# An mLSTM cell with a cosine-gated MLP: the second product by seven half-width block products for eight

## The chip, the cores and the metric

The kernel runs on one core of a Trainium2 chip. The metric is the device time of one execution in microseconds, taken as the median over several runs. The engines are PE (TensorE matmuls; PEld is its weight load), DVE (VectorE), ACT (ScalarE), POOL (GpSimd) and SP (SyncE, which here issues the DMAs). Each engine works off its own instructions strictly in the order in which they were emitted; engines wait for each other through semaphores.

## What is computed

Two stages follow each other. The first is an mLSTM cell over 4 batches, 8 heads, 768 steps and head size 40; the second takes its output as 3072 tokens of width 320 through two matrix products with 2048 hidden columns.

```
for t in range(S):
    m_new = np.maximum(f_gate[:, :, t] + m, i_gate[:, :, t])
    f_stab = np.exp(f_gate[:, :, t] + m - m_new)
    i_stab = np.exp(i_gate[:, :, t] - m_new)
    m = m_new
    C = f_stab[..., None, None] * C + i_stab[..., None, None] * einsum('bhd,bhe->bhde', v_t, k_t)
    n = f_stab[..., None] * n + i_stab[..., None] * k_t
    y[:, :, t] = sigmoid(o_t) * (C q_t) / max(|n . q_t|, 1)
x = y as (4*768, 320)
h = x @ w_in             # 320 x 2048
g = h * cos(h)
out = g @ w_out          # 2048 x 320
```

## The kernel before

The 768 steps are cut into 6 chunks of 128 (`C`), and the cell is computed chunk by chunk in its parallel form: within a chunk by a 128x128 matrix of weights per head, between chunks through a state of 40x48 per head. A *cell* is one chunk of one batch, number n = 4c + b, with all 8 heads, so there are 24 cells. The MLP works on a chunk c of all four batches at once: 512 tokens. The hidden width is cut into 16 blocks of 128 (`f`), taken two at a time, so a chunk has 8 *slots* (`f2` from 0 to 7).

`first_cells` computes the four cells of chunk 0. Then `both_parts(c, b)` runs for every chunk and batch: two slots (i = 0 and 1) of the MLP on chunk c, with the cell of batch b of chunk c + 1 woven in between. The order in which it calls its parts is the order on every engine (the block is under a manual schedule). In chunk 5 there is no cell left to weave in.

A slot with i = 0 emits: `Up` (L605, L608: the first product into two PSUM banks `pup`, six matmuls); `scores` of the cell (L462); for `g` the ACT step `near` (L613) and the DVE step `rest` (L616); `weigh` (L468: scores times decays `E`, DVE); `decay_exponents` of the next cell (L387 DVE subtraction, L388 POOL mask); `sin` (L621, ACT) and `gate` (L625, DVE), which writes `g`; in the first slot of a chunk `sigmoid` of the next chunk's output gates (L316, L318, ACT); `decay` of the next cell (L396, ACT exp); then `down` (L637, the second product) for the slot before; then `turn_gate` (L440, DVE transpose), `values` (L488 to L495, into `vt`), `normalize_turned` (L504 to L515, DVE and POOL), `fade` (L550, POOL) and an ACT instruction that loads the sine's table again (L772). A slot with i = 1 emits `Up`, `seam` (L563: the product `px` that turns a part of y into the MLP's layout; L570: the state's update), `near` and `rest`, `seam_out` (L576), `state` (L588, DVE), `sin` and `gate`, `weigh_k` (L401, POOL), `down`, and the transposes of q and k for the next cell (`turn_blocks` L435, `scale_q` L444).

`down(c, f2)` multiplies the two blocks of g by w_out: for each of the four batches a 128x128 block of g is loaded as weights and 320 columns of w_out stream past it, summed over the 16 blocks in the PSUM banks `po`. The last `down` of a chunk runs in slot 0 of the next, and as each batch ends ACT copies it out (L640) into one of two buffers `o_sb`, and SP stores it (L641). A product in float32 is two passes of the PE, each with its own weight load.

The weights come as 8-byte numbers and are turned to float32 in chunk 0 by `to_float32` (L148 to L156: ACT, DVE, POOL). The maxima for the decays come from DRAM as broadcast tiles: `load_E(n)` (L351) fetches E for two cells at once, 1 MB, and `G` (L356) beside it. The buffers `bits` of the weight conversion are four in pool `pb` and three in pool `pc`. Five small tiles of the gate computation (a1, F1, M1, keep, shift) live in the six buffers of `g`.

Of the kernel before, what the change touches and what calls it, by code (L numbers as in the profile page):

```python
# [11 lines left out]
FP = mybir.dt.float32  # L12
# [3 lines left out]
AF = mybir.ActivationFunctionType  # L16
# [13 lines left out]
def kernel(  # L30
# [23 lines left out]
    C = 128  # L54
# [16 lines left out]
    wp = ctx.enter_context(tc.tile_pool(name="wp", bufs=1))  # L71
    p2 = ctx.enter_context(tc.tile_pool(name="p2", bufs=2))
    p3 = ctx.enter_context(tc.tile_pool(name="p3", bufs=3))
    pe = ctx.enter_context(tc.tile_pool(name="pe", bufs=2))
    p1 = ctx.enter_context(tc.tile_pool(name="p1", bufs=1))
    pb = ctx.enter_context(tc.tile_pool(name="pb", bufs=4))
    pc = ctx.enter_context(tc.tile_pool(name="pc", bufs=3))
# [113 lines left out]
    M0 = gates.tile([BH, C], FP, name="M0")  # L191
    e0 = gates.tile([BH, C], FP, name="e0")
    nM = gates.tile([BH, 1], FP, name="nM")
    a1 = gp.tile([128, WQ], FP, name="a1", tag="g")[0:BH].rearrange("r (c s) -> r c s", c=R)
    F1 = gp.tile([128, WQ], FP, name="F1", tag="g")[0:BH].rearrange("r (c s) -> r c s", c=R)
    M1 = gp.tile([128, WQ], FP, name="M1", tag="g")[0:BH].rearrange("r (c s) -> r c s", c=R)

    keep = gp.tile([128, WQ], FP, name="keep", tag="g")[0:BH].rearrange("r (c s) -> r c s", c=R)
    shift = gp.tile([128, WQ], FP, name="shift", tag="g")[0:BH].rearrange("r (c s) -> r c s", c=R)
    m0 = gates.tile([BH, R], FP, name="m0")  # L200
    dd = gates.tile([BH, R - 1, BH], FP, name="dd")
    nc.gpsimd.memset(keep, 1.0)
# [140 lines left out]

    def load_E(n):
        c, b = divmod(n, B)
        E = pe.tile([128, 2, H, C], FP, name="E", tag="E") if n % 2 == 0 else E2[n // 2]
        if n % 2 == 0:
            E2[n // 2] = E
        if c > 0:
            src = M_d[1][b * H:(b + 2) * H, ts(c - 1, C)]  # L350
            nc.sync.dma_start(out=E.rearrange("q b h t -> q (b h) t"), in_=src.unsqueeze(0).to_broadcast([128, 2 * H, C]))  # L351
            Es[n + 1] = E[:, 1]
            G = p2.tile([128, 2 * HP, C], FP, name="G", tag="G")
            src = G_d.rearrange("(b p j) t -> j (b p) t", j=2, p=HP)
            for j in range(2):
                nc.sync.dma_start(out=G[64 * j:64 * j + 64], in_=src[j, 4 * b:4 * b + 8, ts(c - 1, C)].unsqueeze(0).to_broadcast([64, 2 * HP, C]))  # L356
            Gs[n], Gs[n + 1] = G[:, 0:HP], G[:, HP:2 * HP]
        elif n not in SPREAD:
            nc.sync.dma_start(out=E[:, n % 2], in_=M_d[0][ts(b, H)].unsqueeze(0).to_broadcast([128, H, C]))
        Es[n] = E[:, n % 2]  # L360

    E2 = {}
    pm = {}

    def wall_in(n, i, m):
# [18 lines left out]

    def decay_exponents(n):
        E = Es[n]
        nc.vector.tensor_tensor(out=E, in0=E, in1=cols(n, 0, C), op=OP.subtract)  # L387
        nc.gpsimd.affine_select(out=E, in_=E, compare_op=OP.is_ge, fill=1.0e30, base=0,  # L388
                                pattern=[[0, H], [1, C]], channel_multiplier=-1)

# [2 lines left out]
        nc.vector.tensor_tensor(out=Es[n][:, r], in0=pm[n, i], in1=cols(n, 0, C)[:, r], op=OP.subtract)  # L393

    def decay(n):
        nc.scalar.activation(out=Es[n], in_=Es[n], func=AF.Exp, scale=-1.0)  # L396

    def weigh_k(n):
        if n < N - B:
# [100 lines left out]
    def normalize_turned(n):  # L500
        c, b = divmod(n, B)
        vt = heads_of[n]
        dn = p2.tile([128, C], FP, name="dt", tag="dt")
        nc.vector.tensor_scalar(out=dn, in0=vt[:, 2], scalar1=-TWO_PI, scalar2=TWO_PI, op0=OP.mult, op1=OP.max)  # L504
        nc.vector.scalar_tensor_tensor(out=dn, in0=vt[:, 2], scalar=TWO_PI, in1=dn, op0=OP.mult, op1=OP.max)
        yt = p1.tile([128, 3, C], FP, name="yt", tag="yt")
        nc.vector.tensor_tensor(out=yt, in0=vt, in1=oTs[n], op=OP.mult)
        nc.vector.reciprocal(out=dn, in_=dn)
        db = p1.tile([128, 3, C], FP, name="db", tag="db")
        for i, mask in enumerate(([FROM0] * 32, [FROM1] * 32, [FROM0] * 16 + [FROM1] * 16)):  # L510
            nc.vector.stream_shuffle(out=db[:, i], in_=dn, mask=mask)  # L511
        if b == 0:
            xT[c] = p2.tile([128, NK + 1, B, C], FP, name="xT", tag="xT")
        nc.gpsimd.tensor_tensor(out=xT[c][:, 0:NK, b], in0=yt[:, 0:NK], in1=db[:, 0:NK], op=OP.mult)  # L514
        nc.vector.tensor_tensor(out=yt[:, 2], in0=yt[:, 2], in1=db[:, 2], op=OP.mult)  # L515
        ys[n] = yt

    def normalize(n):
        c, b = divmod(n, B)
# [32 lines left out]
    def seam(n):  # L552

        pool, tag = psum(n)
        if n < B:
            px = pool.tile([128, NK + 1, C], FP, name="px", tag=tag)
            for i in range(NK):
                nc.tensor.transpose(px[:, i], ys[n][:, ts(i, 128)], ident)
            for e in range(2):
                nc.tensor.matmul(px[64 * e:64 * e + 64, NK], ys[n][:, KL:DM], ident, start=True, stop=True)  # L560
        else:
            px = pool.tile([128, C], FP, name="px", tag=tag)
            nc.tensor.matmul(px, pick.rearrange("q e g a i -> q (e g a i)"), ys[n][:, 2], start=True, stop=True)  # L563
        pxs[n] = px
        if n < N - B:
            pu = pool.tile([128, HP, DV], FP, name="pu", tag=tag)
            for p in range(HP):
                for j in range(2):
                    h = 2 * p + j
                    nc.tensor.matmul(pu[64 * j:64 * j + D, p], kws[n][:, h, 0:D], vs(n)[:, h], start=True, stop=True)  # L570
            pus[n] = pu
# [21 lines left out]
    class Up:  # L593
# [27 lines left out]
            nc.scalar.activation(out=r, in_=r, func=AF.Sin, scale=TWO_PI_DOWN)  # L621

        def gate(self, e):
            g = gp.tile([128, WQ], FP, name="g", tag="g")[:, 0:B * C]
            nc.vector.scalar_tensor_tensor(out=g, in0=self.pu[e], scalar=TWO_PI, in1=self.n[e].bitcast(FP),  # L625
                                           op0=OP.mult, op1=OP.mult)
            gs[self.c, 2 * self.f2 + e] = g

    def down(c, f2):
        if f2 == 0:  # L630
            po[c] = [ps_o.tile([128, DM], FP, name="po", tag="o") for _ in range(B)]

        order = [(f, b) for f in (2 * f2, 2 * f2 + 1) for b in range(B)]
        if f2 == NF // 2 - 1:
            order.sort(key=lambda fb: fb[1])
        for f, b in order:
            nc.tensor.matmul(po[c][b], gs[c, f][:, ts(b, C)], w_out_sb[:, f], start=(f == 0), stop=(f == NF - 1))  # L637
            if f == NF - 1:
                o = p2.tile([128, DM], FP, name="o_sb", tag="o_sb")
                nc.scalar.copy(out=o, in_=po[c][b])  # L640
                nc.sync.dma_start(out=out[b * S + c * C:b * S + (c + 1) * C], in_=o)  # L641


    pw, pmu = (ps_u.tile([128, HP, C], FP, name=name, tag="up") for name in ("pw", "pmu"))

# [5 lines left out]
    def first_cells():  # L651
# [64 lines left out]
        weigh_k(2)  # L716
        values(1)
        load_E(B)
        last_rows(1)
        load_o(1)  # L720
        outs.append((0, weights_out(0)))
# [58 lines left out]
    def both_parts(c, b):  # L780
# [3 lines left out]
        for i in range(2):  # L784
# [15 lines left out]
            if i == 0:  # L800
                if cell:
                    weigh(n)
                    if n + 1 < N:
                        decay_exponents(n + 1)
                for e in range(2):
                    up.sin(e)
                    up.gate(e)
                if b == 0 and c + 1 < NC:
                    sigmoid(c + 1)

                if c == 0 and b > 0 and pieces:
                    to_float32(*pieces.pop(0))
                if cell and n + 1 < N and (c > 0 or b > 0):
                    decay(n + 1)
            else:
                if cell:
                    seam_out(n)
                if pieces:
                    to_float32(*pieces.pop(0))
                if cell:  # L820
                    state(n)
                for e in range(2):
                    up.sin(e)
                    up.gate(e)
                while pieces:
                    to_float32(*pieces.pop(0))
                if cell and n + 1 < N:
                    weigh_k(n + 1)
                    odd_values(n + 1)
            if f2 > 0:  # L830
                down(c, f2 - 1)
            elif c > 0:
                down(c - 1, NF // 2 - 1)
            if cell and i == 0:
                turn_gate(n)
                values(n)
# [1 line left out]
                fade(n)  # L838
                if n % 2 == 1 and n + 3 < N:
                    load_two(n + 3, "qk")  # L840
                    load_E(n + 3)
                if b == B - 2 and c + 2 < NC:
                    load_o(c + 2)
# [6 lines left out]
            if i == 1:  # L850
                if c == 0 and b + 2 < B:
                    pieces.extend(weights_in(b + 2))
                for _ in range(min(2, len(outs))):
                    next_out()
                if cell and n + 1 < N:
                    turn_blocks(n + 1)
                    scale_q(n + 1)

    pieces, outs = [], []
    with tc.manual_schedule():  # L860
        first_cells()
        for c in range(NC):
            for b in range(B):
                both_parts(c, b)
        down(NC - 1, NF // 2 - 1)


# [28 lines left out]
```

## Time and profile before

| | us |
|---|---|
| runs before | 581.65, 583.64, 583.67 (median 583.64) |
| the profiled execution | 584.48, span 582.6 |
| PE busy | 553.2 (95%) |
| L637, second product | 223.1 |
| L605 and L608, first product | 176.8 and 54.2 |
| DVE busy | 362.9 |
| ACT busy | 257.1 |
| POOL busy | 150.4 |

Busy times of a group of lines count each moment once, so 768 passes of 445 ns mean come to 223.1 us: the passes overlap. In the profile an arrow `<-` inside square brackets gives the idle time before an instruction and what ended it. Granted clock is the share of full TensorE speed that the chip's throttle allowed.

### The profile page before, as it was taken

The numbers are of one execution on the slowest core, as the hardware profiler recorded it, in microseconds if no ns is written. First come the engines' busy times: TensorE is split into PE (matmuls) and PEld (weight loads), VectorE is DVE, ScalarE is ACT, GpSimd is POOL, SyncE is SP. The second block draws the span as 40 slices with busy tenths as digits, with TensorE's granted clock in tenths as the row PEclk, the third lists the DMA queues.
The fourth block names the chain that finished last, engine by engine and source line by source line (L and its number), as shares of the span: only waits on it lengthen the run. The fifth ranks groups of instructions, "written<-read, shape, count | busy, mean of one in ns | idle before, by whom it ended". The sixth has DMA issues, their size and how long they took to land.

```text
span 582.6 us, 8973 instructions
## 1 busy us (share of the span) xinstructions
PE 553.2 (95%) x3404; PEld 325.7 (56%) x3404; DVE 362.9 (62%) x709; ACT 257.1 (44%) x419; POOL 150.4 (26%) x214
## 2 busy tenths in 40 slices
PE   8994959888999999999999999999999999999997
PEld 5862535444556556556556556566566565555454
DVE  5765798978676766766666667666566585423221
ACT  4856526373364344364343373353274251323222
POOL 7523454543231321321321321321211110000000
PEclk9868889997999999999999999999999999999999
DMA  9999999984805924914914914904810000010001
GB/s 149 221 220 216 229 246 228 198 191 90 153 26 112 161 41 91 154 44 93 160 41 90 154 46 92 182 18 90 154 47 2 0 1 1 0 45 1 0 1 45
DMA packets 125866, 58.76 MB, mean 101 GB/s; under 512 B 61648, under 2 KB 122144, under 8 KB 125824
## 3 DMA queue, kind: packets, MB, share of 16 engines
q1 hardware_dynamic: 125680, 58.00, 50.7%
q8 instruction: 27, 0.44, 0.3%
q0 software_dynamic: 96, 0.18, 0.1%
q14 instruction: 15, 0.12, 0.1%
q10 hardware_dynamic: 48, 0.02, 0.0%
HBM read 54.07 MB, written 5.16 MB: 102 GB/s over the span
## 4 chain that ended last, share of the span: by engine, by line
PE 85%; DVE 5%; DMA 5%; SPq 2%; POOL 2%; issue 1%; ACT 0%; POOLq 0%; DVEq 0%; ACTq 0%
PE po L637 35%; PE pup L605 27%; PE pup L608 8%; PE ps L462 4%; PE vt L495 2%; PE vt L488 2%; DMA E<-M_d 2%; DMA o<-in_o_gate_dram 1%; PE px L563 1%; PE pu L570 1%; DMA ks<-in_k_dram 1%; SPq L140 1%; PE ph L478 1%; PE pt L425 1%; DVE w_out_sb L153 1%
## 5 line engine op out<-in xcount | busy, mean ns | idle before, releaser
L637 PE MATMUL po<-w_out_sb,g 128*128 128x320 f32 x768 | 223.1, 445 | 1.0 <-POOL w_out_sb L156 1.0
L637 PEld LDWEIGHTS po<-w_out_sb,g 128*128 128x128 f32 x768 | 144.5, 193 | 65.8 <-issue 9.5
L605 PE MATMUL pup<-xT,w_in_sb 128*128 128x512 f32 x384 | 176.8, 602 | 1.0 <-POOL w_in_sb L156 0.7
L616 DVE SCALAR_TENSOR_TENSOR n<-pup,n 128x512 f32<-128x512 f32 x96 | 61.7, 685 | 157.6 <-ACT n L613 157.5
L613 ACT ACTIVATE n<-pup 128x512 int32<-128x512 f32 x96 | 51.9, 592 | 235.6 <-PE pup L608 235.6
L605 PEld LDWEIGHTS pup<-xT,w_in_sb 128*128 128x128 f32 x384 | 71.7, 192 | 80.3 <-issue 67.0
L621 ACT ACTIVATE n<-n 128x512 f32<-128x512 f32 x96 | 58.6, 630 | 17.4 <-DVE n L616 15.4
L625 DVE SCALAR_TENSOR_TENSOR g<-pup,n 128x512 f32<-128x512 f32 x96 | 61.6, 684 | 1.7
L388 POOL TENSOR_SCALAR_AFFINE_SELECT E<-E 128x1024 f32<-128x1024 f32 x22 | 24.0, 1092 | 129.2 <-DVE E L387 129.2
L608 PE MATMUL pup<-xT,w_in_l 64*128 64x512 f32 x192 | 54.2, 641 | 0.4 <-POOL w_in_l L156 0.4
L444 POOL TENSOR_TENSOR qG<-t,G 128x512 f32<-128x512 f32 x20 | 25.4, 1272 | 67.3 <-DVE t L435 61.7
L514 POOL TENSOR_TENSOR xT<-yt,db 128x256 f32<-128x256 f32 x20 | 14.5, 725 | 92.7 <-DVE db L511 92.7
L396 ACT ACTIVATE E<-E 128x1024 f32<-128x1024 f32 x24 | 25.4, 1060 | 29.3 <-POOL E L388 28.1
L462 PEld LDWEIGHTS ps<-t,t 40*128 40x128 f32 x384 | 26.5, 199 | 21.0 <-issue 17.8
L462 PE MATMUL ps<-t,t 40*128 40x128 f32 x384 | 28.1, 288 | 10.4 <-DVE t L435 10.4
L608 PEld LDWEIGHTS pup<-xT,w_in_l 64*128 64x128 f32 x192 | 14.4, 184 | 36.8 <-issue 34.9
L468 DVE TENSOR_TENSOR E<-ps,E 128x512 f32<-128x512 f32 x48 | 30.7, 680 | 2.4 <-PE ps L462 2.4
L396 ACT ACT_TABLE_LOAD x21 | 26.9, 1283 | 0.4
L387 DVE TENSOR_TENSOR E<-E,tab 128x1024 f32<-128x1024 f32 x22 | 26.7, 1214 | 0.0
L495 PE MATMUL vt<-qG,st 128*32 128x128 f32 x480 | 24.9, 280 | 0.8 <-POOL qG L444 0.8
L772 ACT ACT_TABLE_LOAD x19 | 24.4, 1283 | 0.2
L550 POOL TENSOR_TENSOR st<-st,tab 40x128 f32<-40x128 f32 x64 | 24.1, 395 | 1.2
(140 smaller groups left out, 510.7 us busy)
## 6 DMA issues: line engine op xcount, KB each, us to landing
E<-M_d SPq DMA_DIRECT2D x10, 1024.0 KB, 5.7
qr<-in_q_dram SPq DMA_DIRECT2D x40, 160.0 KB, 3.5
kr<-in_k_dram SPq DMA_DIRECT2D x40, 160.0 KB, 4.8
G<-G_d SPq DMA_DIRECT2D x20, 256.0 KB, 6.8
bits<-in_moe_w_out_dram SPq DMA_DIRECT2D x8, 640.0 KB, 6.6
bits<-in_moe_w_in_dram SPq DMA_DIRECT2D x32, 128.0 KB, 4.6
out_dram<-o_sb SPq DMA_DIRECT2D x24, 160.0 KB, 1.8
o<-in_o_gate_dram SPq DMA_DIRECT2D x40, 80.0 KB, 3.8
```

The costliest lines, as they stand in the source:

```text
L387: nc.vector.tensor_tensor(out=E, in0=E, in1=cols(n, 0, C), op=OP.subtract)
L396: nc.scalar.activation(out=Es[n], in_=Es[n], func=AF.Exp, scale=-1.0)
L462: nc.tensor.matmul(ps[j][:, p], kT[r, p], qT[r, p], start=True, stop=True)
L468: nc.vector.tensor_tensor(out=w, in0=pss[n][j], in1=w, op=OP.mult)
L495: nc.tensor.matmul(vt[32 * a:32 * a + 32, i], state[:, ts(HP * i + a, 32)], Gs[n][:, a], start=False, stop=True)
L605: nc.tensor.matmul(pu, w_in_sb[:, i, ts(2 * f2 + e, 128)], x(i), start=(i == 0), stop=False)
L608: nc.tensor.matmul(pu, w_in_l[r, f2], x(NK, r), start=False, stop=True)
L613: nc.scalar.activation(out=self.n[e], in_=self.pu[e], func=AF.Copy, bias=0.25)
L616: nc.vector.scalar_tensor_tensor(out=self.n[e].bitcast(FP), in0=self.pu[e], scalar=0.25, in1=self.n[e], op0=OP.add, op1=OP.subtract)
L621: nc.scalar.activation(out=r, in_=r, func=AF.Sin, scale=TWO_PI_DOWN)
L625: nc.vector.scalar_tensor_tensor(out=g, in0=self.pu[e], scalar=TWO_PI, in1=self.n[e].bitcast(FP), op0=OP.mult, op1=OP.mult)
L637: nc.tensor.matmul(po[c][b], gs[c, f][:, ts(b, C)], w_out_sb[:, f], start=(f == 0), stop=(f == NF - 1))
```

## The change

For chunks 1 to 5 the second product is done by Winograd's form of Strassen's scheme. Two blocks f of hidden columns and two batches make a 2x2 array of 128x128 blocks of g; w_out's two blocks of rows and its two halves of 160 columns make a 2x2 array of blocks. Seven products of 128x128 by 128x160 replace eight. The sums on the weights' side (`weight_sums`, POOL, 8 operations of 128x640, with T1 in place of B12) are made once: half in slot 7 of chunk 0, half in slot 0 of chunk 1. Those on the side of g (`sums`) are made in every slot of chunks 1 to 5: four additions of 128x128 on DVE for one pair of batches, four on POOL for the other. The products (`products`) are spread over slots 2 to 7 of a chunk and slot 0 of the next (chunk 1 starts in slot 1). They add up in four banks; a fifth (`late`) takes the two products that have no room, in slot 1 of the next chunk, or in another pool's bank for the last chunk. `combine` and `combine_late` put the parts together on ACT and DVE and store them.

Beside that, `decay_exponents` does no subtraction for chunks 1 to 5: the exp on ACT takes the term a as its bias, one head at a time. The scaling of y is one DVE operation of 128x384, where POOL had 128x256 and DVE 128x128. E is fetched for one cell at a time into three buffers (cell 3 borrows a `bits` buffer), the five gate tiles borrow buffers of q, k and `bits`, and `o_sb` has four buffers.

```
     def load_E(n):
...
+        if n == B - 1:
+            E = pb.tile([128, H, C], FP, name="E3", tag="bits")
+        else:
+            E = pe.tile([128, H, C], FP, name="E", tag="E")
+        Es[n] = E
         if c > 0:
+            nc.sync.dma_start(out=E, in_=M_d[1][ts(b, H), ts(c - 1, C)].unsqueeze(0).to_broadcast([128, H, C]))
+            if n % 2 == 1:
+                return
...
     def decay_exponents(n):
         E = Es[n]
-        nc.vector.tensor_tensor(out=E, in0=E, in1=cols(n, 0, C), op=OP.subtract)
+        if n < B:
+            nc.vector.tensor_tensor(out=E, in0=E, in1=cols(n, 0, C), op=OP.subtract)
...
     def decay(n):
...
+        for h in range(H):
+            g = b * H + h
+            nc.scalar.activation(out=Es[n][:, h], in_=Es[n][:, h], func=AF.Exp, scale=-1.0, bias=tab[:, c, 0, g:g + 1])
...
-        nc.gpsimd.tensor_tensor(out=xT[c][:, 0:NK, b], in0=yt[:, 0:NK], in1=db[:, 0:NK], op=OP.mult)
-        nc.vector.tensor_tensor(out=yt[:, 2], in0=yt[:, 2], in1=db[:, 2], op=OP.mult)
-        ys[n] = yt
+        nc.vector.tensor_tensor(out=xT[c][:, :, b], in0=yt, in1=db, op=OP.mult)
+        ys[n] = xT[c][:, NK, b]
...
+    def weight_sums(part):
...
+        nc.gpsimd.tensor_tensor(out=T3, in0=B22, in1=B12, op=OP.subtract)
+        nc.gpsimd.tensor_tensor(out=B12, in0=B12, in1=B11, op=OP.subtract)
+        nc.gpsimd.tensor_tensor(out=T2, in0=B22, in1=B12, op=OP.subtract)
+        nc.gpsimd.tensor_tensor(out=T4, in0=B21, in1=T2, op=OP.subtract)
+    def sums(c, k):
...
+        tt = nc.vector.tensor_tensor
+        tt(out=S[:, 2], in0=G0[:, 0, 1], in1=G1[:, 0, 1], op=OP.add)
+        tt(out=S[:, 0], in0=S[:, 2], in1=G0[:, 0, 0], op=OP.subtract)
+        tt(out=S[:, 3], in0=G1[:, 0, 0], in1=S[:, 0], op=OP.subtract)
+        tt(out=G0[:, 0, 1], in0=G0[:, 0, 0], in1=G0[:, 0, 1], op=OP.subtract)
+        tt = nc.gpsimd.tensor_tensor
+        tt(out=D1, in0=G0[:, 1, 1], in1=G1[:, 1, 1], op=OP.add)
+        tt(out=S[:, 1], in0=D1, in1=G0[:, 1, 0], op=OP.subtract)
+        tt(out=D4, in0=G1[:, 1, 0], in1=S[:, 1], op=OP.subtract)
+        tt(out=G0[:, 1, 1], in0=G0[:, 1, 0], in1=G0[:, 1, 1], op=OP.subtract)
+    def products(c, k):
...
+        made = [(X0, 0, G0[:, 0, 0], B11), (X0, 1, G1[:, 0, 0], B21), (X0, 2, S[:, 0], T2),
+                (Y0, 0, G0[:, 0, 1], T3), (Y0, 1, G1[:, 0, 1], T4), (Y0, 2, S[:, 2], T1),
+                (Y1, 2, S[:, 3], B22),
+                (X1, 0, G0[:, 1, 0], B11), (X1, 1, G1[:, 1, 0], B21), (X1, 2, S[:, 1], T2),
+                (Y1, 0, G0[:, 1, 1], T3), (Y1, 1, G1[:, 1, 1], T4)]
+        if c == NC - 1:
+            L = late[c]
+            made += [(L, 0, D1, T1), (L, 1, D4, B22)]
...
+    def combine(c, p):
...
+        nc.scalar.copy(out=s[:, 0:HALF], in_=X[:, 0])
+        tt(out=o[0].rearrange("q (h n) -> q h n", h=2), in0=X[:, 1:3], in1=s[:, 0:HALF].unsqueeze(1).to_broadcast([128, 2, HALF]), op=OP.add)
+        if p == 0:
...
+            for e in range(2):
+                out_to(c, e, o[e])
+        else:
+            tt(out=o[1][:, HALF:DM], in0=Y[:, 0], in1=o[0][:, HALF:DM], op=OP.add)
+            tt(out=o[1][:, 0:HALF], in0=Y[:, 1], in1=o[1][:, HALF:DM], op=OP.add)
...
+    def down_slot(c, f2):
+        if c == 0:
+            if f2 > 0:
+                down(0, f2 - 1)
+            return
+        if f2 == 0:
+            if c == 1:
+                down(0, LAST)
+            else:
+                run(made_of[c - 1], 12)
+                combine(c - 1, 0)
+                combine(c - 1, 1)
+            return
+        if f2 == 1 and c > 1:
+            run(late_products(c - 1), NF)
+            combine_late(c - 1)
+            return
...
+        each = 14 if c == NC - 1 else 12
+        quota = [0] * 8
+        for m in range(2, 8):
+            quota[m] = each * 7 * (m - 1) // 6 - each * 7 * (m - 2) // 6
+        run(made_of[c], each if c == 1 else quota[f2])
...
     def both_parts(c, b):
...
+                if c > 0:
+                    sums(c, f2)
...
-            if f2 > 0:
-                down(c, f2 - 1)
-            elif c > 0:
-                down(c - 1, NF // 2 - 1)
+            down_slot(c, f2)
+            if (c, f2) == (1, 0):
+                weight_sums(1)
             if cell and i == 0:
                 turn_gate(n)
                 values(n)
                 normalize_turned(n)
                 fade(n)
                 if n % 2 == 1 and n + 3 < N:
                     load_two(n + 3, "qk")
+                if n + 3 < N:
                     load_E(n + 3)
...
+        run(made_of[NC - 1], 14)
+        for p in range(2):
+            combine(NC - 1, p)
+        combine_late(NC - 1)
```

## The prediction

> **What bounds the kernel now.** I read the page first (shares, costliest groups), then the busy times by stage, the chain of waits around the idle gaps, and the instructions in order of time at one change of token chunk.
>
> ```profile
> PE 553.2 (95%) x3404; PEld 325.7 (56%) x3404; DVE 362.9 (62%) x709; ACT 257.1 (44%) x419; POOL 150.4 (26%) x214
> L637 PE MATMUL po<-w_out_sb,g 128*128 128x320 f32 x768 | 223.1, 445 | 1.0 <-POOL w_out_sb L156 1.0
> ```
>
> ```profile
> 158.80:245.30 86.50, 86.50 (x585) 50.80 (x584) 59.03 (x119) 38.54 (x60) 23.80 (x36) 1.00 0.53 99
> 245.30:331.90 86.60, 86.60 (x586) 50.88 (x585) 57.38 (x117) 38.54 (x60) 22.28 (x35) 1.00 0.52 98
> 502.30:574.30 72.00, 72.00 (x226) 38.24 (x225) 20.61 (x32) 20.00 (x36) 0.00 (x0) 1.00 0.03 10
> ```
>
> The columns of the second fence are window, length, busy us of PE, PEld, DVE, ACT, POOL, granted clock, DMA share, GB/s. From 158.8 us, where the MoE of chunk 1 starts, TensorE is busy all the time at full clock; DVE has a third free. So PE time saved there is saved at the end, unless another engine makes PE wait. The L637 product, which the change rewrites, is 223 us.
>
> **The product itself.** What sets a matmul pass (each f32 product is two)?
>
> ```profile
> 560.87 4.57 PE L637 MATMUL po<-w_out_sb,g 128*128 128x320 f32 x16
> 569.87 8.88 PE L637 MATMUL po<-w_out_sb,g 128*128 128x320 f32 x32
> ...
> 15.71 1.86 PEld L478 LDWEIGHTS ph<-vs,E 128*128 128x128 f32 x16
> ```
>
> Sixteen more passes take 8.88 - 4.57 = 4.31 us: 269 ns for 320 columns. The loads between pup passes of 512 columns stand 0.43 us apart (301.20, 301.63 in the timeline), so a column costs (430 - 269)/192 = 0.84 ns and 160 columns 269 - 134 = 135 ns; I take 136. Weights must be loaded for every pass: sixteen 128-column loads under 41-column passes take 1.86 us, (1.86 - 0.19)/15 = 111 ns apart. That is the floor of a short pass and lies under 136, so loads hide. Ends: 111 ns, and 193 ns (mean length of an L637 load) if nothing of a load hid. Per chunk 64 products x 2 x 0.269 = 34.4 us become 112 x 2 x 0.136 = 30.5. Chunks 1 to 5: **-19.8 us**. Chunk 0 keeps its products.
>
> **The sums of g.** Per slot four DVE and four POOL additions of 128x128. DVE: dependent 128-wide operations stand 0.33 us apart (L504, L505), independent 0.21 (L511): 1.1 us. POOL: 725 ns for 256 columns (L514), 1272 for 512 (L444), so about 0.45 for 128, 1.8 for four; the copy of 128 (L407, 0.30) is the low end, 0.725 the high. But the two sets start together, on the same gate. In the trace L515, a 128x128 product on DVE, takes 0.73 us beside POOL's L514 of 0.73, where 128-wide DVE operations elsewhere take 0.29: it waits for POOL. Locked alternately, DVE's four take 4 x 0.2 + 4 x 0.45 = 2.6 us. I take 2.6. What hides it: in a slot with a cell DVE waited 0.79 us for vt ahead of L504 (170.54), and px was ready 1.0 us early; L387 leaves (1.13 us by its issue), and one 384-wide scaling (0.55, as L507) ends no later than L515 did, less 0.16. PE becomes 0.5 us shorter. Room 0.8 + 1.0 + 1.1 - 0.5 = 2.4 against 2.6: a stall of 0 to 0.2 us for each of 16 cells, 0.3 more in chunk 1 where the slots shrink by 1.0; I count 0 here. With POOL at 0.725 it would be 1 us a cell, 16 us.
>
> The Trainium skill, "SBUF — State Buffer", section "Who interferes with whom", speaks against this part: a DVE instruction with two SBUF inputs and a GpSimd instruction that reads SBUF block each other fully. It agrees with L515; without the rule the sums would cost DVE 1.1 us a slot, with it 2.6.
>
> **Exponents and scaling.** L387 goes (1.21 us of DVE per n), and E no longer waits for DVE before L388. One exp of 1024 (1.06) becomes eight of 128 with a bias: two 128-wide sigmoids (L318) take 0.49, so 0.2 each, 1.7 in all; L224, the one exp with a bias column, takes 0.40, which makes 2.5. I take 2.1. ACT is under half busy; it matters only where something queued behind is awaited, which is the next point. POOL loses L514 (0.73 per n).
>
> **The change of chunk.** Order of before's ACT at the start of chunk 2, and of DVE and PE:
>
> ```profile
> 250.00 1.09 ACT L613 ACTIVATE n<-pup 128x512 int32<-128x512 f32 x2 [7.25 <-PE pup L608]
> 251.35 1.23 ACT L621 ACTIVATE n<-n 128x512 f32<-128x512 f32 x2 [0.27 <-DVE n L616]
> 252.59 1.28 ACT L316 ACT_TABLE_LOAD   x1
> 253.89 1.06 ACT L316 ACTIVATE og<-o 128x1024 f32<-128x1024 f32 x1
> 255.36 1.28 ACT L396 ACT_TABLE_LOAD   x1
> 256.66 1.06 ACT L396 ACTIVATE E<-E 128x1024 f32<-128x1024 f32 x1
> 257.62 0.74 ACT L640 COPY o_sb<-po 128x320 f32<-128x320 f32 x2
> ...
> 254.16 1.28 DVE L625 SCALAR_TENSOR_TENSOR g<-pup,n 128x512 f32<-128x512 f32 x2
> 255.38 0.92 DVE L440 STREAM_TRANSPOSE oT<-og 128x384 f32<-128x384 f32 x1
> 257.10 0.29 DVE L504 TENSOR_SCALAR dt<-vt 128x128 f32<-128x128 f32 x1 [0.80 <-PE vt L495]
> 259.82 0.78 DVE L515 TENSOR_TENSOR yt<-yt,db 128x128 f32<-128x128 f32 x1
> ...
> 261.65 0.49 PE L563 MATMUL px<-yt,pick 128*128 128x128 f32 x2
> ```
>
> The o_sb copies stand behind gates, sigmoids and exps, and nothing but the output waits for them. In the changed kernel the same place holds `combine`: an ACT copy, and eight DVE additions that begin with it, queued on DVE *ahead* of the oT transpose and `normalize_turned`. PE needs the latter for px. On before's clock: the exps end at 256.66 + 2.1 = 258.75; copy 0.29 (between L576's 0.26 and L640's 0.42): 259.05. DVE: 320-wide 0.46 (L528 0.44), 160-wide 0.32, dependent ones 0.03 apart: 2.9 us to 262.0; oT 0.9; from L504 to the end of the shuffles 2.7; scaling 0.58: y at 266.1. PE: pup ends 249.8, scores 1.0, 24 passes and a first load 3.4, vt 1.67, pup and its step to px 4.7: px at 260.5. PE stands **5.5 us** (4.7 to 6.3 by the bounds of exps and additions). With the cell part on, this is at chunks 2, 3 and 4 (chunk 5 has no cell): **+16.5 us**. Behind px queue pu and the late products; DVE's late rest and gates still come before the next pup.
>
> The stall has a price of its own:
>
> ```profile
> 78.50:83.40 4.90, 0.00 (x0) 0.00 (x0) 4.83 (x6) 1.09 (x2) 3.01 (x2) 1.00 1.15 274
> 83.40:90.20 6.80, 6.19 (x24) 4.62 (x25) 5.20 (x8) 1.22 (x2) 2.56 (x3) 0.50 0.88 198
> 131.00:138.00 7.00, 4.73 (x12) 1.74 (x12) 6.86 (x9) 1.63 (x3) 3.49 (x4) 1.00 0.00 0
> 138.00:144.80 6.80, 6.39 (x24) 4.67 (x25) 5.69 (x9) 3.19 (x4) 2.35 (x3) 0.50 1.03 193
> ```
>
> After PE's idle 5.5 us and 2.6 us (waits of scores for L435) the clock was 0.50 for 6.8 us, costing half of 6.2 to 6.4 us of work, 3.1; after waits of 2.1 us it stayed 1.00. A 5.5 us gap is the first kind. In both rows small matmuls (scores) followed; here dense late products come within about 1 us, so full clock may return sooner: I take 2.2 (0 to 3.2) a seam, **+6.6**.
>
> The skill's "TensorE: Matmul & The Clock Gate", Part 1, says that one idle window of some 3.4 us halves the clock and one busy window restores it. By that a seam would cost 1.7; the rows show two windows.
>
> **Smaller parts.** Weight sums: eight POOL operations of 128x640 at 1.58 (L156). The first four end near 167.4, qG 1.3 later, just as vt takes it at 168.98; the second four put fade, then state and gates, late by about 1 us: **+1.2** (0 to 3). Loads: E comes in halves of 512 KB and the odd half goes behind the weights. In 90 to 130 us DMA is full at 214 GB/s, so the w_in piece that ACT awaited for 6.0 us (118.74) comes 2.4 earlier and the 2.1 us px wait at 125.3 shrinks: **-2.0** (-5.3 if the 138 us clock drop also goes, +1 if the extra SP waits bite; each waits for values(n), which ended at 61 us where SP arrives at 78). SP gets ten more E issues of 0.4 us and the last two stores of a chunk, which wait for the late additions; behind them stand loads wanted a slot later or more, so I count nothing, and 1 us a chunk if one is wanted sooner. End: before, the last copy ended 9.5 us after the last pup; now 17 + 14 products (8.5), then late additions and two DMA issues, about 10.5: **+1.0**.
>
> **Sum:** -19.8 + 16.5 + 6.6 + 1.2 - 2.0 + 1.0 = +3.5 us. The profiled execution took 584.48 (span 582.6), 0.8 over the median 583.64; its gaps in chunk 0 vary, so I add to the median and get **587**.
>
> **Rivals.** *The clock stays at the seams* (chance 0.24): seams cost 5.5, the sum is -3.1, 580.5; with chunk 0's other gain 577. It decides at 6.5 us a seam, (19.8 + 2.0 - 2.2)/3: under 5.6 the kernel is faster beyond noise. For it: dense work follows px. Against: two rows of 0.50 after gaps as long or shorter. *The sums lock* (0.14): POOL's 128-wide additions cost over 0.6, px waits 0.5 us in 16 cells: 595. L515 speaks for the lock, POOL's 26% against its size. *No seam stall* (0.07): if DVE's combine does not hold y back, 23 us go: 564. The order of the queues speaks against it. *Passes bound by loads* (0.03): 1120 x 57 ns = +64, 650; the 111 ns spacing is against it.
>
> **How the numbers follow.** Forecast 0.52, its own range 582 to 594. Noise is about 0.5%, 2.9 us. Faster: 0.07 and 0.20 of the first rival, 0.27. Same: 0.04 of it and 0.18 of the forecast, 0.22. Slower: 0.34 + 0.14 + 0.03 = 0.51. Range 576 to 597.
>
> **What would show it.** Passes of 128x160 some 136 ns apart; DVE sums of 0.5 to 0.7 beside POOL's; px waits near 5.5 us for DVE at three chunk starts, with granted clock 0.5 behind each; chunk 1 shortened by about 6 us, chunks 2 to 4 lengthened by about 4 each. Wrong it would be if px never waits, or if cells of other slots wait too.

## The result, and the profile after

The changed kernel took 590.7 us (median; 589.5 to 593.1), the kernel before, beside it on the same chip, 583.65 us. The ratio is 1.0128, with an interval of 1.0081 to 1.0175: slower, by 7 us. Its profiled execution took 591.7 us, span 589.9.

First the page of the changed kernel: its busy times, and two of the five rows of its second product, which was L637 before and is L721 in chunks 1 to 5 now.

```profile
PE 548.5 (93%) x3884; PEld 370.1 (63%) x3884; DVE 421.3 (71%) x904; ACT 279.4 (47%) x549; POOL 219.6 (37%) x362
...
L721 PE MATMUL acc<-w_out_sb,g 128*128 128x160 f32 x320 | 59.0, 305 | 0.0
L721 PE MATMUL acc<-T,g 128*128 128x160 f32 x320 | 58.2, 302 | 0.0
```

TensorE is busy for less time than before (548.5 for 553.2 us; from the start of chunk 1 on 406.4 for 420.0), and for a smaller share of a longer span. DVE went from 62% to 71%. So the passes were saved, and something else grew by more. The busy times chunk by chunk (the windows start where the first product of chunks 1, 2, 3 and 4 starts; columns as before) tell where:

```profile
159.50:240.40 80.90, 79.53 (x642) 52.73 (x641) 64.24 (x142) 43.94 (x88) 45.37 (x65) 1.00 0.54 103
240.40:330.45 90.05, 84.17 (x682) 58.83 (x681) 68.42 (x157) 43.02 (x86) 34.73 (x63) 0.96 0.50 94
330.45:421.55 91.10, 85.22 (x683) 59.88 (x682) 67.93 (x156) 43.02 (x86) 34.27 (x63) 0.96 0.50 93
421.55:508.90 87.35, 81.47 (x618) 57.00 (x617) 66.45 (x139) 37.89 (x76) 23.66 (x42) 0.96 0.07 17
```

Before, these chunks took 86.5, 86.6, 86.6 and 83.9 us, with PE busy all the time at clock 1.00. Chunk 1 is 5.6 us shorter. Chunks 2, 3 and 4 are 3.5, 4.5 and 3.5 longer, each has some 6 us in which PE does nothing, and the clock is no longer 1.00. I call these changes of chunk seams. The chain behind the idle time, in order of time at the start of chunk 2 (start, duration, engine, instruction; in brackets the wait and its releaser):

```profile
250.43 1.28 ACT L402 ACT_TABLE_LOAD   x1
251.73 2.45 ACT L402 ACTIVATE E<-E,tab 128x128 f32<-128x128 f32 x8
254.08 0.27 ACT L737 COPY m<-acc 128x160 f32<-128x160 f32 x1
254.38 0.49 DVE L738 TENSOR_TENSOR o_sb<-acc,m 128x320 f32<-128x320 f32 x1 [3.46 <-ACT m L737]
254.62 1.13 PE L614 MATMUL pup<-xT,w_in_l 64*128 64x512 f32 x4
...
257.28 0.33 DVE L748 TENSOR_TENSOR o_sb<-acc,o_sb 128x160 f32<-128x160 f32 x1
257.52 0.85 DVE L446 STREAM_TRANSPOSE oT<-og 128x384 f32<-128x384 f32 x1
...
260.93 0.56 DVE L521 TENSOR_TENSOR xT<-yt,db 128x384 f32<-128x384 f32 x1
...
261.63 0.77 PE L569 MATMUL px<-xT,pick 128*128 128x128 f32 x2 [5.88 <-DVE xT L521]
```

DVE stands idle for 3.46 us until ACT, busy with a table load and eight exps, makes the copy that `combine` begins with. Then come eight additions (254.38 to 257.6), and only then the oT transpose and the normalization that PE's px needs. PE ends its first product at 255.75 and waits to 261.52. I count a gap from the end of the last matmul to the release of the waiting one: 5.77 us at all three seams (to the start of the px matmul it is 0.1 us more, the 5.88 above). What follows the gap, in the windows of that place:

```profile
255.75:261.50 5.75, 0.00 (x0) 0.00 (x0) 5.47 (x19) 2.73 (x5) 0.00 (x0) 0.73 0.47 150
...
261.50:265.15 3.65, 3.52 (x25) 3.22 (x26) 2.96 (x8) 1.31 (x3) 0.00 (x0) 0.50 0.00 0
265.20:272.00 6.80, 6.80 (x34) 4.69 (x33) 4.46 (x10) 0.00 (x0) 4.31 (x7) 1.00 0.17 54
```

The clock was 0.50 for the first 3.65 us of work behind the gap, though dense products stood there, and then 1.00 again.

### The profile page after: what moved, and what is told of

Same layout as the page of the kernel before. It is cut to its first block, busy times and chain, and to the rows that moved or that the text cites. A ratio compares the mean times of both kernels' runs of the same rounds, so it can differ in the third digit from the quotient of the medians.

```text
span 589.9 us, 10485 instructions
## 1 busy us (share of the span) xinstructions
PE 548.5 (93%) x3884; PEld 370.1 (63%) x3884; DVE 421.3 (71%) x904; ACT 279.4 (47%) x549; POOL 219.6 (37%) x362
## 4 chain that ended last, share of the span: by engine, by line
PE 72%; DVE 12%; ACT 7%; POOL 5%; DMA 2%; issue 2%; DVEq 0%; ACTq 0%; POOLq 0%; SPq 0%
PE pup L611 23%; PE acc L721 21%; PE pup L614 7%; PE late L721 4%; PE ps L468 4%; PE po L643 3%; ACT E L402 2%; PE vt L501 2%; PE vt L494 1%; DMA E<-M_d 1%; DVE t L441 1%; PE px L569 1%; DVE w_out_sb L154 1%; DVE n L622 1%; PE pt L431 1%
## 5 line engine op out<-in xcount | busy, mean ns | idle before, releaser
L685 POOL TENSOR_TENSOR D<-g 128x128 f32<-128x128 f32 x40 | 19.6, 490 | 249.1 <-DVE g L631 223.3
L721 PE MATMUL acc<-w_out_sb,g 128*128 128x160 f32 x320 | 59.0, 305 | 0.0
L721 PE MATMUL acc<-T,g 128*128 128x160 f32 x320 | 58.2, 302 | 0.0
L402 ACT ACTIVATE E<-E,tab 128x128 f32<-128x128 f32 x160 | 49.0, 389 | 4.8 <-POOL E L388 4.6
L721 PEld LDWEIGHTS acc<-w_out_sb,g 128*128 128x128 f32 x320 | 47.4, 190 | 4.0 <-issue 2.3
L721 PEld LDWEIGHTS acc<-T,g 128*128 128x128 f32 x320 | 47.8, 190 | 2.3 <-issue 1.5
L643 PE MATMUL po<-w_out_sb,g 128*128 128x320 f32 x128 | 43.3, 499 | 0.7 <-POOL w_out_sb L157 0.7
L643 PEld LDWEIGHTS po<-w_out_sb,g 128*128 128x128 f32 x128 | 27.5, 221 | 13.5 <-issue 4.7
L721 PE MATMUL acc<-T,S 128*128 128x160 f32 x160 | 35.2, 302 | 0.0
L721 PE MATMUL acc<-w_out_sb,S 128*128 128x160 f32 x160 | 29.0, 300 | 0.0
```

The lines of the kernel that those rows point to most:

```text
L402: nc.scalar.activation(out=Es[n][:, h], in_=Es[n][:, h], func=AF.Exp, scale=-1.0, bias=tab[:, c, 0, g:g + 1])
L721: nc.tensor.matmul(a, lhs, rhs, start=start, stop=stop)
```

## The experiments

How long chunk 0 and the start take differs by some us from one execution to the next (in these traces chunk 1 starts between 153.2 and 162.3 us), so beside the measured times I give lengths from the traces: of a chunk from its first pup pass to the next chunk's, of a slot likewise. Without a wait and at full clock these repeat within 0.02 us. The runs fall into three groups, each with the kernel before beside it (583.04, 584.55 and 585.06 us), so between groups the ratios compare and not the times.

**Where combine stands.** The same additions, emitted behind the normalization instead of ahead of it:

```diff
                 run(made_of[c - 1], 12)
-                combine(c - 1, 0)
-                combine(c - 1, 1)
+                if c == NC - 1:
+                    combine(c - 1, 0)
+                    combine(c - 1, 1)
...
                 sin_next()
+                if f2 == 0 and 1 < c < NC - 1:
+                    combine(c - 1, 0)
+                    combine(c - 1, 1)
```

> The changed kernel with `combine` of chunks 1 to 3 emitted behind normalize_turned and the sine's table load instead of ahead of the oT transpose. Theory (the seam: y waits behind combine, PE idles 5.8 us and then runs 3.4 to 5.7 us at half clock): the three px waits go, -17.3 for the idle and -6.4 for the clock; the late products may now wait about 1 us for combine's first part, the scores behind them as much. 590.7 - 23.7 + 3 = 570 us (567 to 574), granted clock 1.00 from chunk 1 on. Rival (the extra DVE and POOL work is the bound, the order only decides where it shows): the wait moves to the late products or the scores of the same slots, the time stays above 583.

572.44 us, ratio to before 0.9812 (0.9765 to 0.9859): 18 us less than the changed kernel, with not one instruction fewer. Its windows for chunks 2 and 3, then its waits of PE (total, times, longest):

```profile
238.00:321.70 83.70, 83.05 (x683) 57.33 (x682) 68.25 (x157) 43.12 (x86) 34.84 (x63) 1.00 0.53 101
321.70:405.40 83.70, 83.04 (x682) 57.32 (x681) 67.77 (x156) 43.10 (x86) 34.37 (x63) 1.00 0.54 103
```

```profile
PE pup L611 <- DVE g L631: 2.3, 4, 0.9
...
PE px L569 <- DVE xT L521: 0.5, 1, 0.5
```

The px waits of the seams are gone, the clock is 1.00, DVE is busy for as long as in the changed kernel (68.25 against 68.42 us in chunk 2). So it is the place in DVE's queue that cost the time, not the work. What is left of a seam is that slots 1 and 2 are 0.7 and 0.5 us longer than their matmuls alone take (0.6 and 1.1 in chunk 4).

**The exps ahead of the copy.** DVE's queue untouched, but ACT's exps behind combine's copies:

```diff
-                if cell and n + 1 < N and (c > 0 or b > 0):
+                if cell and n + 1 < N and (c > 0 or b > 0) and not (f2 == 0 and c > 1):
                     decay(n + 1)
...
             down_slot(c, f2)
+            if cell and n + 1 < N and f2 == 0 and c > 1:
+                decay(n + 1)
```

> The changed kernel with only the eight exps (and their table load) of the first slot of chunks 2 to 4 moved behind combine's copies on ACT; DVE's order is kept. Theory (two queues in a row: ACT's exps hold the copy, DVE's eight additions hold y): combine starts when the sums end, 250.9 instead of 254.4 in the trace, so each px wait shrinks from 5.8 to about 2.4 us; the clock drop behind it comes only now and then. 590.7 - 10 - (0 to 6) = 575 to 581 us. Rival (DVE's additions alone are the wait): px waits 5 us or more, 588 and above.

575.79 us, ratio 0.9872 (0.984 to 0.9904). The gaps are 2.23, 2.21 and 2.23 us: of 5.77 us, 3.5 were ACT's exps and their table load (as the 3.46 us wait of DVE said), and the 2.2 that are left stand behind the additions. What follows each of the three gaps:

```profile
252.60:259.40 6.80, 6.37 (x36) 6.07 (x37) 5.12 (x13) 2.72 (x7) 2.19 (x5) 0.50 0.00 0
...
341.30:348.20 6.90, 6.90 (x51) 6.62 (x50) 4.87 (x13) 1.85 (x5) 2.95 (x5) 0.75 0.01 2
...
428.00:436.00 8.00, 8.00 (x42) 5.75 (x42) 7.09 (x13) 1.65 (x4) 3.26 (x6) 1.00 0.12 43
```

Three gaps of one length, and the clock fell for 6.8 us, for 3.4 us, and not at all. A short gap is no assurance of full clock.

**The price of the clock.** The gap left as it is, but filled with matmuls that nothing reads:

```diff
+            if n % B == 0 and 2 * B < n:
+                warm(26, px)
+            px = px[:, 0]
             nc.tensor.matmul(px, pick.rearrange("q e g a i -> q (e g a i)"), ys[n], start=True, stop=True)
```

> The changed kernel with 26 idle bf16 matmuls of 512 columns (some 5.6 us) put into PE's queue ahead of px at the three seams; their result is overwritten. They wait for nothing, so px still comes when y comes. Theory (the seam has two prices): the clock stays 1.00, the late products run at 136 ns, 590.7 - 6.4 = 584.3 us (583 to 586), with px no earlier. Rival (the low clock behind the gaps costs nothing that DVE's lateness does not cost anyway): 590 or more.

585.7 us, ratio 1.0015 (0.998 to 1.005). Chunks 2 to 4 became 1.65, 2.69 and 1.63 us shorter, 6.0 in all, at full clock:

```profile
253.00:259.40 6.40, 6.30 (x30) 2.44 (x26) 6.08 (x20) 2.73 (x5) 0.00 (x0) 1.00 0.45 134
259.40:266.00 6.60, 6.59 (x53) 5.73 (x54) 5.68 (x16) 1.31 (x3) 2.95 (x5) 1.00 0.00 0
```

So the stall and its clock add up as two terms, and the clock's is 2.0 us a seam. This also separates the rival "the clock stays at the seams", which fell: in the changed kernel it did not stay.

**One exp for eight.** The subtraction on DVE and the single exp restored in the changed kernel, for all chunks:

```diff
-        if n < B:
-            nc.vector.tensor_tensor(out=E, in0=E, in1=cols(n, 0, C), op=OP.subtract)
+        nc.vector.tensor_tensor(out=E, in0=E, in1=cols(n, 0, C), op=OP.subtract)
...
-        for h in range(H):
-            g = b * H + h
-            nc.scalar.activation(out=Es[n][:, h], in_=Es[n][:, h], func=AF.Exp, scale=-1.0, bias=tab[:, c, 0, g:g + 1])
+        nc.scalar.activation(out=Es[n], in_=Es[n], func=AF.Exp, scale=-1.0)
```

> The changed kernel with the subtraction on DVE and one exp of 1024 restored for all chunks. Theory: the chain exps, copy, additions on DVE sets px at three seams, so the copy starts 1.4 us earlier (one exp 1.06 against 2.45 for eight), the px gap falls from 5.77 to about 4.4 us, the clock still drops behind it: 4.2 us less, 586.5 (585 to 588). Rival: the additions are held by their own queue on DVE (combine first, then the transpose), not by the exps, and DVE gets a further 1.2 us subtraction in each cell: the gap stays at 5 us or more and the time at 590 or above.

594.0 us, ratio 1.0158 (1.012 to 1.0197). Neither expectation holds as a whole. The gaps shrank as the theory had it, to 4.75, 4.40 and 4.39 us, but the time did not. Its waits of PE (px has line 562 here):

```profile
PE px L562 <- DVE xT L514: 20.7, 16, 4.9
```

Sixteen waits for four: beside the seams, 11 slots of chunks 1 to 4 with a cell are now 0.44 to 0.60 us longer. From chunk 1 on, the seams gave back 3.3 us and the other slots took 6.8. The exps became shorter, so the likely cause is the 1.2 us that DVE has more per cell: the sums of g fitted in where the subtraction had been.

**The edits beside the product, alone.** The kernel before, with the halves of E, the exps with a bias and the one scaling of y, but the old product (some of the diff, which is that shown under the change):

```diff
-        nc.vector.tensor_tensor(out=E, in0=E, in1=cols(n, 0, C), op=OP.subtract)
+        if n < B:
+            nc.vector.tensor_tensor(out=E, in0=E, in1=cols(n, 0, C), op=OP.subtract)
...
-        nc.gpsimd.tensor_tensor(out=xT[c][:, 0:NK, b], in0=yt[:, 0:NK], in1=db[:, 0:NK], op=OP.mult)
-        nc.vector.tensor_tensor(out=yt[:, 2], in0=yt[:, 2], in1=db[:, 2], op=OP.mult)
+        nc.vector.tensor_tensor(out=xT[c][:, :, b], in0=yt, in1=db, op=OP.mult)
```

> The kernel before with the side edits alone: E one cell at a time in three buffers, the bias in eight exps without L387, one scaling of y on DVE. The second product stays as it was. Theory of the prediction (chunk 0 gains 2 us because the weights come earlier, the rest is hidden under PE): 583.65 - 2 = 581.6 us (579 to 583). Rival (what chunk 0 gains in one gap it loses in the clock windows, as the profile of the changed kernel has it, where chunk 1 starts 0.7 us later): 583 to 585.

584.53 us, ratio 1.0019 (0.9985 to 1.0053): no gain, within the rival's numbers (that the clock took what a gap gave is not shown by this run). Chunks 1 to 4 are 0.3 us longer each (slot 1 by 0.2, slot 2 by 0.1). Alone the edits are worth nothing; under the sums, the exps with a bias are worth the 0.4 to 0.6 us a slot of the run above.

**All sums on DVE.** The kernel with combine behind, and none of g's sums on GpSimd:

```diff
         tt(out=G0[:, 0, 1], in0=G0[:, 0, 0], in1=G0[:, 0, 1], op=OP.subtract)
-        tt = nc.gpsimd.tensor_tensor
         tt(out=D1, in0=G0[:, 1, 1], in1=G1[:, 1, 1], op=OP.add)
```

> The kernel with combine behind the normalization (572.4), and all eight sums of g on DVE, none on GpSimd. If the two engines lock each other (four of DVE's at 0.42 to 0.50 us and four of GpSimd's at 0.46 to 0.51 alternate and end together after about 2.2 us), then eight on DVE alone at 0.21 to 0.29 us each take 1.7 to 2.3 us: DVE is free again at about the same moment, and the time stays within 1.5 us of that kernel: 571 to 574. Rival: GpSimd's half is a true saving for DVE of four operations a slot, 1 us; then DVE is late by 1 us in each of 16 slots with a cell and of 16 without, TensorE waits for some of them, and the time is 576 or more.

582.45 us, ratio 0.9963 (0.9939 to 0.9987): 10 us more than 572.44 (9.1 from chunk 1 on in the traces), on the rival's side, but mostly not for its reason. In the order of time of the changed kernel, DVE's and GpSimd's halves of one slot:

```profile
298.33 0.46 POOL L685 TENSOR_TENSOR D<-g 128x128 f32<-128x128 f32 x1 [3.93 <-DVE g L631]
298.35 0.58 DVE L680 TENSOR_TENSOR S<-g 128x128 f32<-128x128 f32 x1
298.87 0.46 POOL L686 TENSOR_TENSOR S<-D,g 128x128 f32<-128x128 f32 x1
298.97 0.50 DVE L681 TENSOR_TENSOR S<-S,g 128x128 f32<-128x128 f32 x1
299.40 0.46 POOL L687 TENSOR_TENSOR D<-g,S 128x128 f32<-128x128 f32 x1
299.50 0.50 DVE L682 TENSOR_TENSOR S<-g,S 128x128 f32<-128x128 f32 x1
```

They alternate, one of DVE's after one of GpSimd's, DVE's four in 2.1 us here and in 1.5 us in about half of the slots. Alone on DVE one takes 0.29 us, and eight took 2.2 to 2.7 in every slot but the first: from slot 3 on, chunks 2 to 4 are as long as with the halves, within 0.01 us a slot. There the theory held. In the shorter slots 3, 5 and 7 of chunk 1 the eight cost 0.2 to 0.5 us each, as the rival had it. Most of the loss is where the sums meet other work of GpSimd, around slot 1 of chunk 1 of this kernel:

```profile
173.69 1.67 POOL L668 TENSOR_TENSOR w_out_sb<-w_out_sb 128x640 f32<-128x640 f32 x1
173.88 1.63 DVE L684 TENSOR_TENSOR D<-g 128x128 f32<-128x128 f32 x1
175.44 1.55 POOL L669 TENSOR_TENSOR T<-w_out_sb 128x640 f32<-128x640 f32 x1
175.55 1.59 DVE L685 TENSOR_TENSOR S<-D,g 128x128 f32<-128x128 f32 x1
177.07 1.55 POOL L670 TENSOR_TENSOR T<-w_out_sb,T 128x640 f32<-128x640 f32 x1
177.18 1.59 DVE L686 TENSOR_TENSOR D<-g,S 128x128 f32<-128x128 f32 x1
```

An addition of 0.29 us takes 1.6, as long as the weight sum beside it. Here px waits 5.74 us, the clock is at 0.50 from 181.32 to 188.15 us, and slot 1 is 6.6 us longer, of 7.45 for the whole chunk. The 0.95 us that chunks 2 and 3 lost lie in their slots 1 and 2, behind the seam. With the halves, GpSimd's own four sums stand ahead of the second weight sums in its queue, and DVE is done with its four before these begin (169.0 and 170.2 us in the trace with combine behind): that is what the half was worth. Whether eight sums on DVE would do as well with the weight sums elsewhere, no run shows.

**The weight sums.** The kernel with combine behind, and the eight weight sums behind scale_q:

```diff
-            if (c, f2) == (1, 0):
-                weight_sums(1)
...
-                if (c, f2) == (0, LAST):
-                    weight_sums(0)
                 if cell and n + 1 < N:
                     turn_blocks(n + 1)
                     scale_q(n + 1)
+                if (c, f2) in ((0, LAST), (1, 1)):
+                    weight_sums(c)
```

> The kernel with combine behind the normalization (572.4), and the two halves of the weight sums behind scale_q in GpSimd's order (slot 7 of chunk 0 and slot 1 of chunk 1). Theory: they were late for GpSimd's scale_q, state and fade; the waits of 0.9 and 0.36 us at that place go: 1.3 us less, about 571. Rival: the queue behind the eight operations only shifts the wait to the next consumer (first products, weigh_k): no change, or up to 1 us more.

568.65 us, ratio 0.9726 (0.9697 to 0.9755). In the trace the wait only moved, as the rival had it: slot 1 of chunk 1 went from 10.51 to 8.95 us, slot 3 from 8.95 to 10.22, and all that follows the start of chunk 1 is 0.4 us shorter (410.57 for 410.95). The medians, from two groups, differ by more (ratios 0.9812 and 0.9726). Slot 7 of chunk 0, which the edit also touches, is 9.99 us in both traces, so the rest is not explained; chunk 0 varies by as much from one execution to the next. Then the four of chunk 1 were cut in two, behind slots 1 and 3, and with them combine's second half went to slot 1:

```diff
                 if f2 == 0 and 1 < c < NC - 1:
                     combine(c - 1, 0)
-                    combine(c - 1, 1)
...
+                if f2 == 1 and 1 < c < NC - 1:
+                    combine(c - 1, 1)
...
-                if (c, f2) in ((0, LAST), (1, 1)):
-                    weight_sums(c)
+                if (c, f2) == (0, LAST):
+                    weight_sums(0)
+                if c == 1 and f2 in (1, 3):
+                    weight_sums(1, (f2 // 2,))
```

> The kernel with the weight sums behind scale_q (568.7), and two waits that its trace still shows cut up: the second half of combine goes from the first slot of a chunk to behind the sums of the second slot, and the second four weight sums go two behind slot 1 and two behind slot 3 of chunk 1. Theory: what is left at a seam (slots 1 and 2 longer by 0.7 and 0.5 us in chunks 2 and 3, by 0.6 and 1.1 in chunk 4) is DVE's combine ahead of the next gates, so about half of these 4.1 us goes, and 0.6 of the 1.3 us that slot 3 of chunk 1 lost: 2 to 3 us less, 566 (565 to 567), chunks 2 and 3 near 83.1. Rival: DVE is as late in the second slot (state, gates and sums stand there too), the waits only change place: within 1 us of 568.7.

569.94 us, ratio 0.975 (0.97 to 0.9799): not to be told from the one before. Its windows of chunks 1 and 2:

```profile
159.90:239.10 79.20, 79.20 (x641) 52.68 (x640) 63.11 (x142) 43.93 (x88) 45.21 (x65) 1.00 0.54 103
239.10:322.80 83.70, 82.79 (x682) 57.32 (x681) 68.10 (x157) 43.08 (x86) 34.76 (x63) 1.00 0.54 105
```

Chunk 1 has no wait left. It is 1.3 us shorter than in the run before and 1.7 us shorter than in the changed kernel, the whole price of the weight sums. Chunk 2 is where it was: slot 1 is 0.71 us shorter and slot 2 0.70 us longer, the rival's case. These two kernels are the fastest, 2.7% and 2.5% under the kernel before.

**Chunk 0.** The kernel before, with more matmuls that nothing reads in the gaps of chunk 0:

```diff
+        if B < n < 2 * B:
+            warm(25 if n == B + 1 else 10, ps[0])
...
-                    warm(8, psum_o())
+                    warm(34, psum_o())
```

> The kernel before with more matmuls that nothing reads in the gaps of chunk 0 (34 for 8 ahead of one values, 25 and 10 ahead of three scores). Theory: the half-clock windows behind these gaps cost up to 3.1 us each and their number varies from execution to execution; with the gaps filled they go: 3 to 9 us less, 575 to 581, and a smaller spread. Rival: the waits behind the gaps are for other engines and a transfer, and full-speed PE only arrives earlier at the next wait: less than 1.5 us.

583.83 us, ratio 0.9993 (0.9963 to 1.0023): nothing, as the rival had it. In the trace the waits of the scores are filled and no clock drop stands behind them, but px waits 5.95 us at 124 us, and the clock is at 0.50 from 128.95 to 135.78 us. In that stretch ACT waits for a piece of w_in, in this kernel (first line) for longer than in the kernel before (second):

```profile
123.76 0.66 ACT L148 ACTIVATE w_in_sb<-bits 128x512 f32<-128x512 f32 x1 [9.85 <-DMA bits<-in_moe_w_in_dram]
...
118.74 0.67 ACT L148 ACTIVATE w_in_sb<-bits 128x512 f32<-128x512 f32 x1 [6.00 <-DMA bits<-in_moe_w_in_dram]
```

PE was not early here (its scores began at 112.19 us, for 111.11 in the kernel before). SP issued the piece 4.9 us later (116.48 for 111.55 us), and from the issue to ACT's instruction it took as long, 7.3 for 7.2 us. In 70 to 130 us of the kernel before the DMA engines are busy throughout (share 1.08, 217 GB/s). That these transfers and SP's queue pace chunk 0, and not PE's clock, fits; no run here thinned the transfers out or changed their order.

## Why the prediction was right, point by point

The forecast, 587 us and slower, was right in sign and mechanism; 590.7 is 3.7 above it. All the terms but the last can be read against the slots of the changed kernel's trace:

| term | predicted | measured |
|---|---|---|
| product, chunks 1 to 5 | -19.8 | a slot with 12 products 8.95 for 9.99 us (24 x 0.136 - 16 x 0.269 = -1.04), with 14 products 9.49 for 9.99 (-0.50): as predicted |
| px gap at three seams | +16.5 | 3 x 5.77 = +17.3 |
| clock behind it | +6.6 | +6.3 |
| weight sums, and what else chunk 1 lost | +1.2 | +1.7 |
| end | +1.0 | last slot to the end 18.52 for 17.34: +1.2 |
| from chunk 1 on | +5.5 | 430.41 - 423.86 = +6.55 |
| loads of chunk 0 | -2.0 | +0.1 |

The clock's +6.3 is what is left of slot 1 in chunks 2, 3 and 4 (17.57, 18.59, 16.88 us, where their matmuls alone make 10.04, 10.04 and 9.37; the excess is 23.6 in all) when the gaps are taken off.

**Product.** The 0.84 ns a column from two widths gave the spacing of a third, 136 ns, and loads hid. "Passes bound by loads" fell.

**The seam.** The queue order was read rightly, copy behind exps, additions ahead of oT. With the additions moved the gap went, and with the exps moved 2.2 of 5.77 us were left. Within the gap one size was off: the exps were taken as 2.1 us and took 2.45, on the high bound, which the one row with a bias column (L224, 0.40) had given. The skill's page "ScalarE: Activation LUTs", section "What ACT_TABLE_LOAD costs", has 280 ns + 0.833 ns a column for an operation with a bias column, overlapping by 93 ns; by that the estimate is 8 x 387 - 7 x 93 = 2.45 us, what the trace has. "No seam stall" fell.

**Clock.** I took 2.2 us a seam and the filled gap gave back 2.0; the first rival fell on it. But the size came out right partly by luck. I expected the dense products to bring full clock back sooner; in fact the clock was at 0.50 for 6.83 us at each seam, as in the two rows of the prediction. It cost 1.8, 2.8 and 1.7 us because 3.3, 1.2 and 3.5 us of it fell into the gap, where PE ran nothing.

The reason I gave in passing, that waits of 2.1 us leave the clock alone, was wrong as a rule: of three gaps of 2.2 us two were followed by half clock. The skill's "TensorE: Matmul & The Clock Gate", Part 1, says that activity is judged in windows of some 3.4 us that run freely. Drops of 3.4 and 6.8 us behind equal gaps agree with that; its rule that one busy window restores the clock holds at the changed kernel's first seam (3.65 us of work at 0.50), but not behind the first gap of 2.2 us (0.50 for 6.8 us, PE busy for 6.4 of them).

The traces show which gaps drop the clock. In each of the eleven, all changes of the clock lie whole multiples of 3.41 us apart. Cut into such windows from 60 us on, they give this: every window at full clock in which PE was idle for 1.86 us or more was followed by half clock (36 of 36), none with under 1.47 us was, and of the 9 between two were. Of the three gaps of 2.2 us the fullest windows held 1.95, 2.31 and 1.59 us of idle time: the third gap was split over two windows, and the clock stayed.

**Sums.** The locked alternation was as predicted, though shorter (1.5 to 2.1 us for my 2.6). From chunk 1 on one cell outside the seams waited, for 0.46 us in slot 1 of chunk 1. That 0 for the cells needed L387's departure, as the text said: with L387 back 11 slots lost 0.44 to 0.60 us each. "The sums lock" fell on its size: GpSimd's additions took 0.46 to 0.51 us, and it needed over 0.6.

**The term that failed** is chunk 0: "the w_in piece that ACT awaited for 6.0 us (118.74) comes 2.4 earlier and the 2.1 us px wait at 125.3 shrinks: -2.0". The waits did what it says. ACT waits 3.90 us for that piece in the changed kernel, px does not wait any more, and slot 5 of chunk 0 became 2.70 us shorter (9.99 for 12.69). But slot 4 became 3.08 us longer (17.20 for 14.12). The scores and the product of that slot, in the kernel before, then, with the piece of w_in, in the changed kernel:

```profile
111.11 1.16 PE L462 MATMUL ps<-t,t 40*128 40x128 f32 x16 [2.21 <-DVE t L435]
112.20 4.57 PE L637 MATMUL po<-w_out_sb,g 128*128 128x320 f32 x16
...
111.82 2.08 PE L468 MATMUL ps<-t,t 40*128 40x128 f32 x16 [2.13 <-DVE t L441]
113.83 6.82 PE L643 MATMUL po<-w_out_sb,g 128*128 128x320 f32 x16
...
117.35 0.66 ACT L149 ACTIVATE w_in_sb<-bits 128x512 f32<-128x512 f32 x1 [3.90 <-DMA bits<-in_moe_w_in_dram]
```

Two gaps of one length; behind the second the clock was at 0.50 (111.57 to 118.39 us). So in this execution the gain of one gap went into a clock drop behind another. What the term left out is, once more, that gaps of 2.1 us can drop the clock.

Over all runs the gain is not there either. Take each kernel's median less its trace from chunk 1 on, less the same of the kernel before beside it: for the nine kernels with E in halves this gives 0.5, 2.3, -2.0, 2.1, 1.7, 0.5, -2.6, -0.6 and -0.5 us, a mean of +0.1 with a standard error of 0.6 (from one trace each). What took it in the other executions stays open: in three of the nine traces the clock does not drop at that place. The prediction's sum was +3.5 us and the result +7.05; of the difference 1.05 us lie from chunk 1 on and 2.5 in chunk 0 and the start.

## What to carry to other kernels

When a product is cut by an algebraic scheme, look first at which queue its extra additions enter and who waits behind them: here the same instructions, placed behind the normalization, turned 1.3% slower into 1.9% faster. A PE gap costs its length and then, depending on how it falls on the clock's windows of 3.41 us, up to some 3 us of half clock, so a gap of 2 us is not safe either. An edit that is worth nothing alone may be the room that another one needs, so undo it in the company it is meant for.

## What the runs showed of the hardware that was not expected

A DVE addition of 128x128 with both inputs in SBUF stretched from 0.29 us to the whole length of the GpSimd operation beside it, 0.46 to 0.58 us beside additions of 128x128 and 1.6 us beside those of 128x640: the cost of sharing is set by the other engine's operation, not by one's own. An exp of 128x128 with a bias column took 389 ns, eight in a row 0.29 us apart, so splitting one exp of 1024 (1.06 us) into eight costs 1.4 us. And the clock drop behind a gap of 2.2 us lasted 6.8, 3.4 or 0 us in one execution: what counted was how much of the gap lay in one window of 3.41 us (1.95 and 2.31 us dropped the clock, 1.59 us did not).
